# One SBUF tile with a table of places, and thirty groups of gates and values by seven products

## The chip, the cores and the metric

The kernel runs on one core of one Trainium2 chip. The metric is device time in microseconds. Before the change it is 280.34 us, the median of three runs (279.88 to 280.62). Half precision (f16) is used for most operands, PSUM sums are f32.

## What is computed

Attention over 4 sequences of 768 positions with 8 heads of 64, in which each query looks only at 6 of its 24 chunks of 32 keys, and then a gated feed-forward layer over the 3072 tokens:

```python
k_min, k_max = min and max of k over each chunk of 32 keys
ub = sum(maximum(q * k_min, q * k_max))          # bound of each chunk, future chunks at -1e9
top_chunks = argsort(ub)[..., -6:]
attn = softmax(where(chunk in top_chunks and causal, q @ k.T / sqrt(64), -1e9))
x = (attn @ v) as [3072, 512]
gate = sigmoid(x @ w_gate); val = x @ w_val      # 512 x 1536 each
out = (gate * val) @ w_out                       # 1536 x 512
```

## The kernel before, in words

The 24 blocks of 128 tokens are grouped into eight units (u0 to u7) of 384 tokens. For each unit the kernel prepares keys and queries (transposes, chunk minima and maxima, copies into `hk` and `hq`), chooses the chunks (`choose`), attends (`attend`: scores at line 937, exponentials at 948, the causal mask at 954, values at 970, then `finish` divides and turns the result into `xT`), and runs the feed-forward layer (`ffn`, line 1223). The feed-forward of one unit stands beside the attention of the next.

All work is registered with a planner (`Plan.add`) as steps with the engines they may run on. The order of all steps and the engine of each are written out in the string `ORDER`; `SLOTS` names for each buffer the slot it uses, and `TIES` adds waits, each of a GpSimd step for a VectorE step. `Plan.order` only reads these strings. Each engine runs its own steps in the order in which they stand.

`ffn` makes gates and values in groups of four feature blocks (`q4`), three groups of each a unit. The long way (`whole`, line 1230) is 4 matmuls of 384 columns for each feature block. Where `SEVEN` names the group, `by7` (line 1181) splits the 512 x 512 weights and the 512 x 384 inputs into halves and forms the four quarter results from seven products in place of eight (Winograd's form of Strassen's method):

```python
product("p7", side, ...); product("p1", lead, ...)
move("e7", side, f7); product("p4", side, ...)
move("e4", side, f4); move("sd", lead, side)
product("p6", lead, ...); onto("c21", f4); product("p2", side, ...)
product("p5", lead, ...); onto("c22", f7); product("p3", lead, ...)
```

`side` and `lead` are two PSUM banks. A product (line 1190) is 4 matmuls of 192 columns. `move` (line 432 or 434) copies a bank to SBUF or to the other bank, on ScalarE or VectorE; `onto` (line 1205) adds `lead` to `f4` or `f7` on VectorE. Products use sums of weights (`ss`, line 1158, four for each group's weights, made once) and differences of inputs (`tt`, line 1173, four a unit). Then come four tanh steps (`squash`, line 1243) for gates and four gating steps (`gated`, line 1249) for values. `SEVEN` holds the gates of unit 5 and the gates and values of units 6 and 7: 15 groups.

The last layer of units 4 to 7 (`pair`, line 1046) is by seven products too: once over two blocks of a unit, and once over the third blocks of two units (u45, u67; the earlier unit's third blocks are kept in `held`). Its sums lie in `sw` or `sx`, the weight sums in `tw` (line 1033), and the four result blocks in a part of `sw`, or for u45 and u67 in `ox`; they are scaled on the way (lines 1040, 1042, 1088) and stored (line 1110). Other units use the long way (`o`, line 1313).

SBUF buffers come from tile pools with a number of slots for each kind (line 415: 2 `big`, 6 `v`, 7 `np`, 9 `hg` and so on). Weight sums and differences have no slots of their own: they lie in areas whose first use is over (`homes`, `t_`, and the kind `nq`, which lies in `hk[0]`), and `done_with` adds the waits for the earlier use. `weight_sums` waits for the keys of sequence 3 (line 1403).

Of the kernel before, what the change touches and what calls it, by code (L numbers as in the profile page):

```python
# [14 lines left out]
NEG = -60000.0  # L15

# [22 lines left out]
class Plan:  # L39
# [3 lines left out]
    def __init__(self, slots, caps):  # L43
        self.slots, self.caps = slots, caps
        self.ops = []
        self.writer, self.readers = {}, {}
# [80 lines left out]
kx0_u2_1=V kx0_u2_3=V kx1_u2_3=V kx1_u2_2=V kx0_u2_2=V qm_u2_3=V kcr_u2=V ub_u2=P qf16_3=V kt_u2_3=A kf16_3=V osb_u0_1=A scf_3=P  # L127
expf_3_0=A out_u0_0=S vc_3=G hk1_u2_1=G hk0_u2_0=V hk0_u2_3=G kt_u2_2=A g_u1_1=P tanh_u1_1=A g_u1_0=P cmf_3_0=G ubn1_u2=V ubn0_u2=V
mx1_u2=V k11_1=S k00_1=S k10_1=S g_u1_8=P mx0_u2=V g_u1_4=P ap1_u2=V v_u1_0=P ap0_u2=V tanh_u1_4=A k01_1=S apt1_u2=V tanh_u1_0=A apt0_u2=V
expf_3_1=A hqm0_u2_0=A hqm1_u2_0=G v_u1_4=P v_u1_1=P sc_u2_4_1=P hg_u1_4=V q11_1=S sc_u2_5_2=P tanh_u1_8=A q01_1=S q10_1=S exp_u2_5_2=A  # L130
q00_1=S exp_u2_4_1=A pvf_3_0=P rzf_3_0=V out_u0_1=S cmf_3_1=G v16_0_5=G xf_3_0=V g_u1_5=P sc_u2_4_0=P sc_u2_1_2=P v16_0_4=G tanh_u1_5=A
sc_u2_5_1=P v_u1_5=P hg_u1_0=V hk1_u2_3=G pvf_3_1=P sc_u2_4_2=P sc_u2_5_0=P v_1_3=S hg_u1_1=V ss0_g0=V hqm0_u2_2=G exp_u2_4_0=A
sc_u2_0_2=P exp_u2_1_2=A rzf_3_1=V g_u1_3=P hq1_u2_2=G exp_u2_5_1=A sc_u2_1_0=P hg_u1_5=V xf_3_1=V exp_u2_5_0=A exp_u2_4_2=A g_u1_6=P
exp_u2_0_2=A hk0_u2_2=G kx1_1_2=V sc_u2_1_1=P xpsf_3_0=P kx0_1_1=V sc_u2_0_0=P o0_u0_2=P k16_1_3=A o1_u0_2=P v_1_0=S cm_u2_4=G
exp_u2_1_0=A sc_u2_0_1=P exp_u2_1_1=A kx0_1_3=V cm_u2_5=G exp_u2_0_0=A v_u1_3=P kx0_1_2=V kx1_1_1=V hqm1_u2_2=G hk1_u2_2=G sc_u2_6_2=P
tanh_u1_6=A k16_1_2=G o2_u0_2=P cm_u2_1=G cm_u2_0=G tanh_u1_3=A hg_u1_3=V sc_u2_6_0=P v_u1_6=P ss0_g1=G kx0_1_0=V exp_u2_0_1=A pv_u2_1=P
osb_u0_2=A g_u1_10=P hq0_u2_3=G ss1_g1=G kx1_1_0=V exp_u2_6_0=A kx1_1_3=V sc_u2_3_0=P hg_u1_6=V exp_u2_6_2=A v_u1_8=P pv_u2_0=P hg_u1_8=V
k16_1_0=G k16_1_1=A rz_u2_0=V g_u1_7=P exp_u2_3_0=A hq1_u2_3=G xTf_3_0=A kt_1_0=V x_u2_0=V qf0_u3_2=V k00_2=S sc_u2_3_1=P exp_u2_3_1=A
tanh_u1_7=A sc_u2_7_0=P pv_u2_5=P sc_u2_7_1=P sc_u2_2_2=P pv_u2_4=P k01_2=S kt_1_3=V sc_u2_7_2=P exp_u2_7_1=A k10_2=S sc_u2_2_1=P
qf0_u3_3=V v_u1_10=P exp_u2_7_0=A sc_u2_3_2=P rz_u2_2=V x_u2_2=V exp_u2_2_1=A g_u1_9=P kcr_1=G cm_u2_3=G exp_u2_2_2=A qf0_u3_0=V cm_u2_6=G  # L140
qf0_u3_1=V tanh_u1_10=A tanh_u1_9=A g_u1_2=P qm_u3_2=G exp_u2_3_2=A tanh_u1_2=A qf0_u4_1=V sc_u2_6_1=P v_u1_7=P g_u1_11=P v_u1_2=P
hq1_u3_0=G qm_u3_0=A kt_1_1=V hk1_1_0=G v_1_1=S v_u1_9=P exp_u2_7_2=A cm_u2_7=G ub_u3=P hg_u1_10=V hq1_u3_2=A hg_u1_7=V sc_u2_2_0=P
exp_u2_2_0=A v_u1_11=P exp_u2_6_1=A hg_u1_2=V o0_u1_2=P qf0_u4_0=V hk1_1_3=G xps_u2_2=P xpsf_3_1=P xT_u2_2=A v16_1_3=G o1_u1_2=P
hq0_u3_0=G ubn1_u3=V ubm1_u3=V cm_u2_2=G mx1_u3=V kt_1_2=V hg_u1_9=V pv_u2_7=P o0_u1_1=P ap1_u3=V apt1_u3=V pv_u2_3=P qf0_u4_2=V ubn0_u3=V
pv_u2_6=P pv_u2_2=P k11_2=S tanh_u1_11=A hg_u1_11=V xTf_3_1=A hk1_1_1=G hqm1_u3_0=A sc_u3_4_2=P hqm1_u3_2=A sc_u3_5_2=P exp_u3_5_2=A
# [12 lines left out]
tanh_u2_7=A hg_u2_9=V sc_u3_2_2=P exp_u3_2_2=A v_u2_1=P v_u2_3=P hk0_2_1=G ubn1_u4=V cm_u3_1=G sc_u3_3_2=P tanh_u2_10=A sc_u3_2_0=P
qf0_u5_2=V qm_u5_0=A rz_u3_2=V exp_u3_2_0=A ubn0_u4=V v_2_1=S sc_u3_3_0=P exp_u3_3_2=A hg_u2_1=V cm_u3_0=G cm_u3_2=G g_u2_3=P ubm0_u4=V
hk0_2_2=G pv_u3_0=P k11_3=S mx0_u4=V sc_u3_1_1=P exp_u3_1_1=A sc_u3_2_1=P exp_u3_3_0=A v_u2_7=P ap0_u4=V tanh_u2_3=A exp_u3_2_1=A v_u2_2=P  # L160
g_u2_6=P apt0_u4=V g_u2_5=P hg_u2_3=V hk1_2_1=G hqm0_u4_0=A tanh_u2_6=A v16_1_5=G cm_u3_3=G ubm1_u4=V v_u2_5=P hg_u2_2=V sc_u4_0_2=P
tanh_u2_5=A exp_u4_0_2=A v16_2_0=G hqm0_u4_2=G pv_u3_1=P x_u3_2=V hg_u2_7=V hq1_u5_0=G sc_u4_0_3=P exp_u4_0_3=A sc_u4_1_3=P v_u2_10=P
sc_u4_1_2=P k10_3=S hg_u2_5=V qm_u5_2=A v_u2_6=P sc_u4_0_1=P exp_u4_1_2=A rz_u3_0=V x_u3_0=V hg_u2_10=V sc_u4_1_0=P v16_2_1=G mx1_u4=V
sc_u4_0_0=P xT_u3_2=S exp_u4_1_0=A exp_u4_0_0=A exp_u4_0_1=A ap1_u4=V pv_u3_3=P sc_u4_2_3=P pv_u3_2=P rz_u3_1=V cm_u4_0=G sc_u4_2_0=P
x_u3_1=V exp_u4_1_3=A hk1_2_3=G hq1_u4_0=G o0_u2_0=P sc_u4_2_2=P xT_u3_1=S hg_u2_6=V exp_u4_2_3=A hq1_u4_2=G sc_u4_1_1=P exp_u4_2_0=A
sc_u4_3_0=P kx1_3_3=V pv_u4_0=P exp_u4_3_0=A apt1_u4=V kx0_3_0=V sc_u4_3_1=P exp_u4_1_1=A k16_3_2=G exp_u4_3_1=A qf0_u6_0=V ub_u5=P
ubn1_u5=V sc_u4_3_3=P cm_u4_1=G hqm1_u4_0=A v_3_3=S k16_3_0=G cm_u4_2=G sc_u4_3_2=P exp_u4_3_2=A sc_u4_2_1=P mx1_u5=V o1_u2_0=P o2_u2_0=P
exp_u4_2_2=A hqm1_u4_2=A ubn0_u5=V qf0_u6_3=V xT_u3_0=S osb_u2_0=V g_u3_0=P k16_3_1=G kt_3_0=V pv_u4_1=P sc_u4_7_3=P sc_u4_4_2=P g_u3_5=P
rz_u4_0=V exp_u4_3_3=A qf0_u6_1=V sc_u4_7_0=P sc_u4_7_2=P tanh_u3_0=A exp_u4_4_2=A sc_u4_4_1=P v_u3_0=P qf0_u6_2=V exp_u4_7_3=A cm_u4_3=G
# [212 lines left out]
def kernel(  # L382
# [741 lines left out]
    def flat(t):  # L1124
        return t.rearrange("p a s -> p (a s)")
# [221 lines left out]
    for i in range(3):  # L1347
        weights_out(i, 0.3, [])
# [113 lines left out]
```

## Time and profile before

| | |
|---|---|
| median of 3 runs | 280.34 us (279.88 to 280.62) |
| profiled execution | 279.69 us, span 277.9 us |
| TensorE (PE) / weight loads (PEld) | 266.3 / 195.8 us busy |
| VectorE (DVE) / ScalarE (ACT) / GpSimd (POOL) | 220.7 / 202.4 / 159.0 us busy |
| granted TensorE clock | 1.00 |

The profile shows one execution. The span runs from its first to its last instruction. A busy time is the time in which an engine has at least one instruction under way. Matmuls are pipelined, so a record (326 ns for a matmul of 384 columns) is longer than the time by which it moves the next one on. The chain is the work that ended last, followed back from the last instruction. A group of instructions gives line, engine, operation, output and input, count, then busy time, mean ns of one, and the engine's idle time just before them with its releaser.

### The profile page before, as it was taken

What the parts mean: (1) busy time and instruction counts of PE and PEld (TensorE: products, weight loads), DVE (VectorE), ACT (ScalarE), POOL (GpSimd) and SP (SyncE); (2) the same over time, 40 slices, a digit from 0 to 9 for tenths busy, and PEclk for the clock granted to TensorE, in tenths of its full rate; (3) what the DMA queues carried; (4) which work ended last, traced back from release to release, by engine and by line L of the source; (5) the groups of instructions that cost most, each with busy time, mean ns of one, the idle gap of its engine ahead of it and who ended that gap; (6) DMA issues with size and microseconds to landing.
All of it is one profiled execution on the core that took longest, in us unless ns stands there. A gap on an engine that the chain in (4) does not pass through costs nothing.

```text
span 277.9 us, 7782 instructions
## 1 busy us (share of the span) xinstructions
PE 266.3 (96%) x2914; PEld 195.8 (70%) x2914; DVE 220.7 (79%) x649; ACT 202.4 (73%) x436; POOL 159.0 (57%) x254
## 2 busy tenths in 40 slices
PE   6968999999999999999999999999999999999993
PEld 4744658666756566757667656767986899999982
DVE  4798845769989998999896889557868568879872
ACT  6387869659777877888886998767877695576441
POOL 5797644648778666884847545531553765251621
PEclk9999999999999999999999999999999999999999
DMA  7999999999998999958843205300302030010315
GB/s 160 242 270 198 201 215 214 211 192 188 206 191 180 193 216 179 163 113 173 139 108 88 80 0 120 92 0 2 96 4 78 0 84 17 0 40 1 116 42 188
DMA packets 131574, 34.72 MB, mean 125 GB/s; under 512 B 119760, under 2 KB 128464, under 8 KB 131536
## 3 DMA queue, kind: packets, MB, share of 16 engines
q1 hardware_dynamic: 126768, 29.50, 50.4%
q0 software_dynamic: 4768, 4.72, 10.1%
q8 instruction: 23, 0.38, 0.6%
q14 instruction: 15, 0.12, 0.1%
HBM read 30.67 MB, written 6.29 MB: 133 GB/s over the span
## 4 chain that ended last, share of the span: by engine, by line
PE 88%; DMA 6%; POOL 1%; SPq 1%; ACT 1%; DVE 1%; issue 0%; DVEq 0%; ACTq 0%
PE v_u L1236 16%; PE g_u L1236 14%; PE sc_u L937 13%; PE o_u L1313 11%; PE pv_u L970 7%; PE pl_g_u L1190 4%; PE pl_u L1065 4%; PE ps_u L1065 4%; PE ps_g_u L1190 3%; PE ube_u L876 3%; DMA wg<-in_moe_w_gate_dram 3%; PE pl_v_u L1190 3%; PE ps_v_u L1190 2%; DMA out_dram<-ox 1%; DMA qf<-in_q_dram 1%; SPq L616 1%
## 5 line engine op out<-in xcount | busy, mean ns | idle before, releaser
L948 ACT ACTIVATE att_u<-sc_u 128x512 f16<-128x512 f32 (+3 forms) x184 | 91.0, 552 | 17.2 <-PE sc_u L937 12.6
L1236 PE MATMUL v_u<-xT_u,wv 128*128 128x384 f16 x288 | 55.6, 326 | 0.0
L1236 PE MATMUL g_u<-xT_u,wg 128*128 128x384 f16 x240 | 46.7, 326 | 1.7 <-DMA wg<-in_moe_w_gate_dram 0.8
L954 POOL TENSOR_SCALAR_AFFINE_SELECT att_u<-att_u 128x384 f16<-128x384 f16 (+1 forms) x56 | 27.9, 508 | 28.9 <-ACT att_u L948 16.8
L1249 DVE SCALAR_TENSOR_TENSOR hg_u<-gate_u,v_u 128x384 f16<-128x384 f16 x60 | 32.2, 543 | 14.8 <-PE v_u L1236 6.6
L1243 ACT ACTIVATE gate_u<-g_u 128x384 f16<-128x384 f32 x60 | 29.1, 500 | 13.4 <-PE g_u L1236 13.1
L1236 PEld LDWEIGHTS <-wv 128*128 128x128 f16 x288 | 27.2, 98 | 14.5 <-issue 0.2
L1313 PE MATMUL o_u<-wo,hg_u 128*128 128x512 f16 x144 | 35.0, 379 | 0.0
L1236 PEld LDWEIGHTS <-wg 128*128 128x128 f16 x240 | 22.0, 98 | 14.9 <-DMA wg<-in_moe_w_gate_dram 2.5
L937 PE MATMUL sc_u<-hqo,hko 128*128 128x128 f16 (+2 forms) x220 | 29.2, 243 | 0.0
L937 PE MATMUL sc_u<-hqe,hke 128*128 128x128 f16 (+2 forms) x220 | 28.7, 243 | 0.0
L970 PE MATMUL pv_u<-v,att_u 128*128 128x65 f16 x640 | 27.4, 193 | 0.0
L970 PEld LDWEIGHTS <-att_u 128*128 128x128 f16 x640 | 25.1, 98 | 2.9
L937 PEld LDWEIGHTS <-hke 128*128 128x128 f16 x220 | 17.2, 98 | 6.9 <-issue 2.0
L1313 PEld LDWEIGHTS <-hg_u 128*128 128x128 f16 x144 | 13.4, 98 | 12.1
L937 PEld LDWEIGHTS <-hko 128*128 128x128 f16 x220 | 16.8, 98 | 5.8 <-issue 0.4
L653 POOL CAST v<-v 128x512 f16<-128x512 f32 x23 | 14.1, 613 | 7.7 <-PE sc_u L937 2.6
L991 DVE TENSOR_TENSOR x_u<-pv_u,rz_u 128x384 f16<-128x384 f32 (+1 forms) x28 | 14.8, 529 | 0.4
L1205 DVE TENSOR_TENSOR f_g_u<-pl_g_u,f_g_u 128x384 f32<-128x384 f32 x18 | 9.9, 553 | 4.0 <-PE pl_g_u L1190 3.6
L1190 PEld LDWEIGHTS <-ss 128*128 128x128 f16 x144 | 12.4, 98 | 0.7
L899 DVE MAX8 mx_u<-ubn_u 128x8 f32<-128x8 f32 (+16 forms) x152 | 12.6, 158 | 0.1
L1055 POOL TENSOR_TENSOR sw<-hg_u 128x256 f16<-128x256 f16 x7 | 4.7, 670 | 13.6 <-DVE hg_u L1249 8.0
(246 smaller groups left out, 612.7 us busy)
## 6 DMA issues: line engine op xcount, KB each, us to landing
v<-in_v_dram SPq DMA_DIRECT2D x23, 256.0 KB, 3.6
k<-in_k_dram SPq DMA_DIRECT2D x12, 384.0 KB, 5.4
q<-in_q_dram SPq DMA_DIRECT2D x12, 384.0 KB, 5.6
out_dram<-osb_u SPq DMA_DIRECT2D x12, 256.0 KB, 2.9
out_dram<-sw SPq DMA_DIRECT2D x8, 256.0 KB, 2.2
wv<-in_moe_w_val_dram POOLq DMA_DIRECT2D x3, 512.0 KB, 10.7
wo<-in_moe_w_out_dram POOLq DMA_DIRECT2D x3, 512.0 KB, 17.8
qf<-in_q_dram SPq DMA_DIRECT2D x8, 128.0 KB, 3.4
```

Source lines behind the costliest of these rows:

```text
L653: plan.add(f"v16_{b}_{ib}", {POOL: pool(H * D)}, lambda e: nc.gpsimd.tensor_copy(v16[b % 2][:, ib, :, 0:D], at(t)), reads=[t], writes=[("v ...
L937: nc.tensor.matmul(at(t)[:, o:o + 128 * m], hk[b % 2][e_][:, p, 128 * jb:128 * jb + 128], hq[u.side][e_][:, p, 128 * x:128 * (x + m)], sta ...
L948: plan.add(f"exp_{u.name}_{h}_{y}", {ACT: act(n)}, lambda e, t=t, att=att, b0=b0, n=n: nc.scalar.activation(at(att)[:, b0:b0 + n], at(t), ...
L954: nc.gpsimd.affine_select(out=dv, in_=dv, compare_op=ALU.is_ge, fill=0.0, base=0, pattern=[[0, u.m], [1, 128]], channel_multiplier=-1)
L970: nc.tensor.matmul(at(pv)[:, last, x, :], at(att)[:, c:c + 128], v16[b % 2][:, jb, h, :], start=(jb == 0), stop=(jb == ib))
L991: plan.add(f"x_{u.name}_{p}", {DVE: dve(u.t)}, lambda e: nc.vector.tensor_tensor(at(x_).rearrange("p a (e d) -> p e a d", e=2), at(pv)[:, ...
L1065: nc.tensor.matmul(at(to), a(j)[:, i], b(j)[:, i], start=first and j == i == 0, stop=j == 2 and i == 1, skip_group_check=True)
L1190: nc.tensor.matmul(at(to)[:, s], a()[:, c, 128 * s:128 * s + 128], b()[:, c], start=first and s == c == 0, stop=c == 1, skip_group_check=True)
L1236: nc.tensor.matmul(at(t), w16[:, c, 128 * fb:128 * fb + 128], at(u.xt)[:, c, :], start=(c == 0), stop=(c == 3))
L1243: made = plan.add(f"tanh_{u.name}_{name}", {ACT: act(T, psum)}, lambda e: nc.scalar.activation(dst(), src(), AF.Tanh, scale=0.5), reads=re ...
L1249: plan.add(f"hg_{u.name}_{name}", {DVE: dve(T)}, lambda e: nc.vector.scalar_tensor_tensor(dst(), gate(), 1.0, src(), ALU.add, ALU.mult), r ...
L1313: nc.tensor.matmul(at(o), at(hgs[fc // 2])[:, fc % 2, 128 * tb:128 * tb + 128], wo16[:, fc, lo:hi], start=(fc == 0), stop=(fc == NFB - 1))
```

## The change

All passing SBUF buffers become ranges of one tile, the arena: 234 places of 256 f16 elements a partition, and `SLOTS` gives each buffer its first place. PSUM buffers stay as they are. Ranges may be used one after the other by buffers of any kind. `ss`, `tt`, `held`, `sums`, `four` and the gates of the seven products are now buffers of their own; the areas in `hk`, `hq`, `v16`, the explicit waits (`done_with`, the wait of `weight_sums`), and the shared `sw`, `sx`, `ox` are gone. `att` buffers take as much as their unit needs.

`SEVEN` grows from 15 groups to 30: gates and values of units 3, 4 and 5 are added where they were missing.

`ORDER`, `SLOTS` and `TIES` are written anew; the first 425 entries of `ORDER` are the same. Steps by engine, before and after: PE 686 and 731, DVE 503 and 538, ACT 435 and 471, POOL 248 and 260, SP 127 and 127. Ties: 163 and 190. The order of `tw` (weight sums of the last layer), registered earlier, is in `ORDER` still at units 4 and 5; the 24 steps of `ss` end in it before the products of unit 4. The copies `move` are on VectorE 9 times of 45 before and 22 of 90 after.

```diff
-    plan = Plan(
-        {"ps": 8, "big": 2, "v": 6, "np": 7, "qf": 2, "qm": 1, "kx": 2, "kt": 3, "ubn": 1, "mx": 1, "apt": 1,
-         "att": 4, "rz": 2, "x": 3, "xt": 2, "gate": 4, "hg": 9, "osb": 2, "nq": 6},
-        {("ps", "ff"): 4, ("ps", "sc"): 3, ("ps", "pv"): 2, ("ps", "pr"): 3, ("ps", "ub"): 2},
-    )
+    plan = Plan()
+    UNIT = 256
+    arena = land.tile([128, UNITS * UNIT], F16, tag="arena", name="arena")

     def at(b):
...
+            t = arena[0:b.shape[0], UNIT * b.slot:UNIT * b.slot + n * (2 if b.dtype == F32 else 1)]
+            if b.dtype == F32:
+                t = t.bitcast(F32)
...
-            att = Buf("att", f"att_{u.name}_{h}", [128, 1920], F16)
+            att = Buf("att", f"att_{u.name}_{h}", [128, 128 * len(u.where)], F16)
...
-    tw = Buf("big", "tw", [128, 4, 3, 2, 256], F16)
-    sw = Buf("big", "sw", [128, 3072])
-    held = Buf("qm", "held", [128, 2, NFB, 128], F16)
-    sx = Buf("qf", "sx", [128, 3, 4, 2, 128], F16)
-    ox = Buf("qf", "ox", [128, 4, 256])
+    tw = Buf("tw", "tw", [128, 4, 3, 2, 256], F16)
...
-    def pair(name, block, keys, sums, four, skey, okey, rows, next_):
+    def pair(name, block, keys, rows, next_):
...
+        skey = Buf("sums", f"sums_{name}", [128, 3, 4, 2, 128], F16)
+        okey = Buf("four", f"four_{name}", [128, 4, 256])
...
-    SEVEN = {5: {"g": (0, 1, 2)}, 6: {"g": (0, 1, 2), "v": (0, 1, 2)}, 7: {"g": (0, 1, 2), "v": (0, 1, 2)}}
+    SEVEN = {3: {"g": (0, 1, 2), "v": (0, 1, 2)}, 4: {"g": (0, 1, 2), "v": (0, 1, 2)}, 5: {"g": (0, 1, 2), "v": (0, 1, 2)}, 6: {"g": (0, 1, 2), "v": (0, 1, 2)}, 7: {"g": (0, 1, 2), "v": (0, 1, 2)}}
...
     for m in "gv":
         for i in range(3):
+            b = Buf("ss", f"ss_{m}{i}", [128, 4, 512], F16)
+            ss[m, i] = [((b, x), lambda b=b, x=x: at(b)[:, x]) for x in range(4)]
...
+        tt = Buf("tt", f"tt_{u.name}", [128, 4, 2, T2], F16)
...
-                gate = [Buf("nq", f"gq_{u.name}_{2 * q4 + f}", [128, 2, T], F16) for f in range(2)]
+                gate = [Buf("gq", f"gq_{u.name}_{2 * q4 + f}", [128, 2, T], F16) for f in range(2)]
...
+                u.held = Buf("held", f"held_{u.name}", [128, NFB, 128], F16)
...
+    weight_sums(0.4)
     prepare(units[1], 0.0, 0.8)
...
-    summed = weight_sums(4.9)
     attend(units[4], 4.0)
...
-    turned_k = [op for op in plan.ops if op.name.startswith("kt_3_")]
-    for op in summed:
-        op.deps += [(d, False) for d in turned_k]
```

At the end of the kernel the pairs run interleaved: unit 6, unit 7 and u67. Before, the last matmuls are those of u67; after, those of unit 7. In the new `SLOTS` the results `four` of u45 stand at place 214 and those of u67 at 198, eight places each.

More of the change, by code (lines that the diff above doesn't have):

```diff
@@ L130 @@
[L130 to L133, printed above, removed]
@@ L1042, in halved, with sums, four @@
             nc.vector.tensor_scalar_mul(o, i, 0.5)
-    def pair(name, block, keys, sums, four, skey, okey, rows, next_):
+    def pair(name, block, keys, rows, next_):
         EV = 0.1
+        skey = Buf("sums", f"sums_{name}", [128, 3, 4, 2, 128], F16)
+        okey = Buf("four", f"four_{name}", [128, 4, 256])
+        def sums(n, j):
+            return at(skey)[:, j, n]
+        def four():
+            return at(okey)
         for j in range(3):
@@ L1112, in store @@
             dma=((hi - lo) * 1.35, 2048 if hi - lo > 256 else 512))
[L1114 removed]
+    SEVEN = {3: {"g": (0, 1, 2), "v": (0, 1, 2)}, 4: {"g": (0, 1, 2), "v": (0, 1, 2)}, 5: {"g": (0, 1, 2), "v": (0, 1, 2)}, 6: {"g": (0, 1, 2), "v": (0, 1, 2)}, 7: {"g": (0, 1, 2), "v": (0, 1, 2)}}
     T2 = T // 2
[L1116 to L1136 removed]
     ss = {}
[L1138 to L1139 removed]
+    for m in "gv":
+        for i in range(3):
+            b = Buf("ss", f"ss_{m}{i}", [128, 4, 512], F16)
+            ss[m, i] = [((b, x), lambda b=b, x=x: at(b)[:, x]) for x in range(4)]
     made7 = set()
@@ L1147, in halves, with xt_keys @@
         return lambda: view().rearrange("p (i f) -> p i f", i=2)
+    def xt_keys(u):
+        return [(u.xt, c) for c in range(4) if u.m] + [(u.xt, c, x) for c in range(4) for _, x in u.first]
     def sums_of(u, next_):
@@ L1172, in sums_of @@
                                     (lambda: x_(1, 1), lambda: x_(0, 1)), (lambda: x_(1, 0), lambda: t_(1)))):
-            made = plan.add(f"tt{n}_{u.name}", {DVE: dve(384, 2), POOL: pool2(384)}, lambda e, a=a, b=b, n=n: both(e).tensor_tensor(
-                t_(n), a(), b(), ALU.subtract), reads=[(u.xt, c) for c in range(4)] + [(tk, n // 2)] * (n % 2), writes=[(tk, n)], port=True, prio=next_())
-            done_with(made, keys0 if u.i == 5 else [("hq", u.side, 0, n), ("hqm", u.side, 0, n), ("hqm", u.side, 0, n, "zero")])
-        return t_, x_
+            plan.add(f"tt{n}_{u.name}", {DVE: dve(384, 2), POOL: pool2(384)}, lambda e, a=a, b=b, n=n: both(e).tensor_tensor(
+                t_(n), a(), b(), ALU.subtract), reads=xt_keys(u) + [(tt, n // 2)] * (n % 2), writes=[(tt, n)], port=True, prio=next_())
+        return t_, x_, tt
     def by7(u, m, i, next_, views):
-        t_, x_ = views
+        t_, x_, tt = views
         name = f"{m}{i}_{u.name}"
@@ L1206, in onto @@
                      reads=[lead, f], writes=[f], prio=next_(0.1))
-        xs = [(u.xt, c) for c in range(4)]
+        xs = xt_keys(u)
         product("p7", side, sum_(2), lambda: t_(2), tk(2, 2), True)
@@ L1227, in ffn @@
         hgs = []
-        xt = [(u.xt, c) for c in range(4) if u.m] + [(u.xt, c, x) for c in range(4) for _, x in u.first]
+        xt = xt_keys(u)
         def whole(m, fb):
@@ L1242, in squash @@
         def squash(name, src, dst, psum, reads, writes):
[L1243 to L1246 removed]
+            plan.add(f"tanh_{u.name}_{name}", {ACT: act(T, psum)}, lambda e: nc.scalar.activation(dst(), src(), AF.Tanh, scale=0.5),
+                     reads=reads, writes=writes, prio=next_(EV))
         def gated(name, gate, src, dst, psum, reads, writes):
```

529 lines of the change are left out of this document (265 added, 264 removed).

## The prediction

> **What bounds the kernel now.** I read the page first, then the stretches of 20 us, then the chain. A busy TensorE alone proves little, since its records overlap, so the pace within the chain decides.
>
> ```profile
> span 277.9 us, 7782 instructions
> PE 266.3 (96%) x2914; PEld 195.8 (70%) x2914; DVE 220.7 (79%) x649; ACT 202.4 (73%) x436; POOL 159.0 (57%) x254
> PE   6968999999999999999999999999999999999993
> PE 88%; DMA 6%; POOL 1%; SPq 1%; ACT 1%; DVE 1%; issue 0%; DVEq 0%; ACTq 0%
> ```
>
> ```profile
> 60.00:80.00 20.00, 20.00 (x189) 13.80 (x188) 18.10 (x35) 17.77 (x39) 14.70 (x25) 1.00 1.13 193
> 80.00:100.00 20.00, 20.00 (x194) 11.91 (x192) 18.29 (x55) 14.34 (x31) 15.82 (x25) 1.00 1.06 195
> 100.00:120.00 20.00, 20.00 (x270) 14.00 (x269) 18.58 (x66) 16.99 (x37) 13.91 (x22) 1.00 0.85 161
> 120.00:140.00 20.00, 20.00 (x241) 13.17 (x237) 18.94 (x59) 16.83 (x36) 14.29 (x21) 1.00 0.78 148
> 140.00:160.00 20.00, 20.00 (x256) 13.35 (x255) 16.46 (x63) 16.16 (x30) 11.65 (x17) 1.00 0.39 96
> 160.00:180.00 20.00, 20.00 (x236) 13.07 (x234) 16.54 (x56) 16.76 (x32) 10.92 (x15) 1.00 0.31 74
> 180.00:200.00 20.00, 20.00 (x221) 15.15 (x219) 14.14 (x38) 14.65 (x32) 6.61 (x11) 1.00 0.11 29
> 200.00:260.00 60.00, 60.00 (x706) 54.25 (x704) 46.61 (x117) 43.39 (x104) 26.53 (x40) 1.00 0.10 30
> 260.00:278.00 18.00, 13.20 (x126) 11.72 (x123) 10.31 (x30) 4.90 (x14) 6.75 (x11) 0.99 0.33 125
> ```
>
> The columns are length, busy PE, PEld, DVE, ACT and POOL with their instructions, granted clock, DMA share and GB/s. From 60 to 260 us TensorE is busy all the time at a granted clock of 1.00, and 88% of the chain is TensorE. VectorE is second: 90 to 95% in the stretches from 60 to 140 us. ScalarE reaches 89%, GpSimd 79%. After 200 us only TensorE is full. The DMA transfers stand in the chain at the head and in the tail.
>
> ```profile
> 212.98 2.60 PE v_u L1236 x16
> 215.58 0.66 PE ps_g_u L1190 x8
> 216.24 0.22 PE sc_u L937 x2
> ```
>
> These are three neighbours in the chain: start, length, line and number of matmuls. 212.98 + 2.60 = 215.58 and 215.58 + 0.66 = 216.24: one piece starts where the other ends, and TensorE waits for nobody. So a matmul of 384 columns costs 2.60 / 16 = 0.163 us of TensorE and one of 192 columns 0.66 / 8 = 0.0825 us, and each microsecond of matmuls taken out is a microsecond of the end, as long as TensorE stays fed.
>
> **The change part by part.**
>
> *Products.* Four feature blocks of gates or values for 384 tokens take 16 matmuls of 384 columns (L1236): 16 x 0.1625 = 2.60 us. By seven products they take 28 of 192 columns (L1190): 28 x 0.0825 = 2.31 us. That is 0.29 us less for each group. SEVEN grows from 15 groups to 30: six of unit 3, six of unit 4, the three value groups of unit 5. 15 x 0.29 = 4.35 us leave TensorE (240 long matmuls out, 420 short ones in). All 15 lie in the stages where TensorE is full: **minus 4.35 us**.
>
> *What the products need around them.* Each group has two additions on VectorE (c21, c22; L1205) and three moves out of PSUM (e7, e4, sd; ScalarE or VectorE). The tanh and the gating stay four each, of 384 elements a partition.
>
> ```profile
> L1205 DVE TENSOR_TENSOR f_g_u<-pl_g_u,f_g_u 128x384 f32<-128x384 f32 x18 | 9.9, 553 | 4.0 <-PE pl_g_u L1190 3.6 <-ACT ox L1040 0.3
> L434 DVE COPY f_g_u<-ps_g_u 128x384 f32<-128x384 f32 x3 | 1.7, 554 | 0.2 <-PE ps_g_u L1190 0.2
> L1158 DVE TENSOR_TENSOR ss<-wg x5: 408/418/426, 64.4 to 190.2; 128x512 f16<-128x512 f16 x5
> L1173 DVE TENSOR_TENSOR hqe<-xT_u,hqe 128x384 f16<-128x384 f16 x3 | 1.1, 353 | 0.0
> ```
>
> The order that is written out names the engine of every step, so it can be counted. VectorE goes from 503 steps to 538. It gains 30 additions (30 x 0.553 = 16.6 us), 13 moves (22 instead of 9; 13 x 0.554 = 7.2 us) and 3 differences of x (11 instead of 8; 1.1 us). It loses 7 weight sums to GpSimd (11 instead of 18; 7 x 0.418 = 2.9 us) and, net, 4 smaller copies, about 2 us. Sum: about 20 us more for VectorE. ScalarE goes from 435 to 471:
>
> ```profile
> L432 ACT COPY f_g_u<-ps_g_u 128x384 f32<-128x384 f32 x15 | 7.0, 482 | 6.4 <-PE ps_g_u L1190 6.2 <-ACT hke L1243 0.2
> L1158 POOL TENSOR_TENSOR ss<-wg x1: 1149/1149/1149, 69.7 to 69.7; 128x512 f16<-128x512 f16 x1
> ```
>
> 32 more moves on it are 32 x 0.482 = 15.4 us. GpSimd goes from 248 to 260, with seven more sums of 1.149 us (8.0 us); it is the idlest of the four, and its 27 more ties (190 instead of 163, each a GpSimd step that waits for a VectorE step) hold up only GpSimd's own queue.
>
> *Is that covered?* From 60 to 200 us VectorE is busy 18.10 + 18.29 + 18.58 + 18.94 + 16.46 + 16.54 + 14.14 = 121.05 us of 140. With 20 us more it is 141.0 of 140 - 4.35 = 135.65. Taken as they stand, 5.4 us have no room: the upper end of the cost. But a record's last part is overlapped by the next record:
>
> ```profile
> 99.55 0.97 DVE L827 STREAM_TRANSPOSE kt<-k 128x768 f16<-128x768 f16 x1
> 100.44 0.94 DVE L661 TRANSPOSE_TENSOR_REDUCE kx<-k 128x24 f32<-128x768 f32 x1
> ```
>
> The second starts 0.08 us before the first ends. For the 372 instructions of the seven stretches that is up to 30 us that the busy time counts twice or as a tail, so the room is there, and the lower end is 0. It isn't below nothing: TensorE has no idle time there that a better order could take away. The nearest row is 120 to 140 us: VectorE 18.94 of 20 and TensorE still 20.00. That speaks for the lower end; that a whole stage of 135 us would now look like its fullest stretch speaks against exactly 0. I take **plus 1.0 us**, a fifth of the upper end.
>
> *The places.* Buffers that were rotating tiles are now ranges of one tile, given by the table. No byte is moved more: 127 SyncE steps before and after. The first 425 entries of the order are unchanged, which covers the head, so I count the places at nothing there. A write to a range that is still read has to wait, as it had to wait for a tile; the cover is the same as above. Weight sums used to wait for dead areas (line 1403 for keys, done_with for others); now all 24 of `ss` stand in the order ahead of unit 4's products. That moves work, and its cost is in the counts.
>
> *The tail.* One wait is removed, and here the profile shows it:
>
> ```profile
> 269.76 4.04 DMA out_dram<-ox
> 272.38 0.82 PE L1065 MATMUL pl_u<-wo,sx 128*128 128x256 f16 x6
> 273.90 0.43 DVE L1042 TENSOR_SCALAR ox<-ps_u 128x256 f32<-128x256 f32 x1 [1.81 <-DMA out_dram<-ox]
> 273.91 0.38 ACT L1040 ACTIVATE ox<-pl_u 128x256 f32<-128x256 f32 x1 [1.55 <-DMA out_dram<-ox]
> 274.39 0.33 SPq L1110 DMA_DIRECT2D out_dram<-ox  x1
> ```
>
> The pairs u45 and u67 share the buffer ox. The last two evacuations must wait until the store of u45 has read it, at 273.80, though the last matmul ends at 273.20. After the change the four blocks of u45 lie at places 214 to 221 and those of u67 at 198 to 205, which do not meet. What is late next is the last matmul itself: 273.20, then about 0.1 to start, 0.38 for the copy, 0.1 to the issue, and 277.9 - 274.39 = 3.51 from issue to the end, which gives 277.29 instead of 277.9: **minus 0.6 us**. (The order now ends with unit 7 in place of u67, with the same kinds of step.)
>
> *Sum.* The profiled execution took 279.69 us, of which 277.9 is its span. 279.69 - 4.35 - 0.6 + 1.0 = 275.74, which is 3.95 less. The median of the three runs is 280.34, 0.65 above the profiled one; 280.34 - 3.95 = **276.4 us**.
>
> [...]
>
> **The rivals.**
>
> *VectorE becomes the bound.* For it: the 141.0 of 135.65 above. Against it: the overlap of its records, and that its next largest jobs, the key extremes and transposes of 0.95 us, are needed a stage later. If the 5.4 us all come through: 279.69 - 4.95 + 5.4 = 280.1, against the median 280.8. No gain.
>
> *The hand-offs get uncovered (slower).* Two PSUM banks serve a group, and TensorE may not refill one before e7, e4, sd, c21 or c22 has emptied it: five hand-offs a group, 75 more. One that nothing covers costs the rest of the last matmul's record and the copy, 0.246 - 0.0825 + 0.482 = 0.65 us:
>
> ```profile
> L1190 PE MATMUL pl_g_u<-hqe,ss 128*128 128x192 f16 x48 | 5.9, 246 | 0.0
> L1190 PEld LDWEIGHTS <-ss 128*128 128x128 f16 x144 | 12.4, 98 | 0.7
> ```
>
> It decides from 4.95 / 75 = 0.066 us a hand-off on average, that is, when one in ten stands bare. With 15% bare it is 75 x 0.15 x 0.65 = 7.3 us: 279.69 - 4.95 + 7.3 = 282.0, median 282.7. For it: in units 3 and 4 the copies queue on a VectorE and a ScalarE that are far fuller than after 200 us. Against it: most of the groups of today run from 200 to 260 us, and TensorE is busy 60.00 of 60 there, with an idle time before L1190 of 0.0; and units 3 and 4 have scores and values of the next unit to run in between.
>
> *Weight loads set the pace.* If each short matmul had to wait for its load of 98 ns, a group would take 28 x 0.098 = 2.74 us, 0.14 more than the long way: 279.69 + 15 x 0.14 - 0.6 + 1.0 = 282.2, median 282.8. Against it stands 0.66 us for eight of them, and loads that overlap. [...]
>
> **How the numbers follow.** Forecast (products shorter, nearly all covered, tail wait gone), 275.0 to 278.6: 0.78. More than forecast, down to 274.6 or below: 0.02. VectorE the bound, about 280.8: 0.08. Hand-offs bare, about 282.7: 0.10. Weight loads, about 282.8: 0.02. The range of 274.5 to 279.4 leaves out the last three, under 2 in 10, and reaches from no cost of the cover (275.4) with some room to four times the cost taken. A difference of 0.3% (0.84 us) is about what a measurement can tell from no change. Faster by more than that 0.81, within it 0.07, slower 0.12: the forecast, the larger gain and an eighth of the VectorE case are faster, the rest of that case is about the same, and the other two are slower.
>
> **What would show it.** In the changed profile: L1236 left with 288 matmuls and the line of the seven products with 840, eight of these still in 0.66 us; TensorE busy 20.00 in every stretch from 60 us to some 4 us earlier than now; VectorE near 240 us in all, with stretches at 19 and more; no wait of an evacuation for a store of the four blocks in the last 5 us. The forecast is wrong if TensorE shows idle time before the products, released by VectorE or ScalarE copies (hand-offs), or if the key transposes come late and scores wait for them (VectorE the bound), or if loads of weights from the new places space the matmuls wider than 0.0825 us.

## The result, and the profile after

After the change the kernel takes **291.19 us**, the median of four runs (289.58 to 293.07), against 280.48 of the kernel before on the same chip: a ratio of 1.038 (95% interval 1.030 to 1.046). The forecast was 276.4. The kernel became slower by 10.7 us where 3.95 less were forecast. Of the kernels in this document some executions last over 1.5% longer than the fastest of the same kernel (one of the kernel with eleven copies on ScalarE took 951.96 us): the ratios leave these out, the medians keep them.

The page of the changed kernel, the lines that answer to those of before; the row with q1 is the queue of the loads, with packets, megabytes, and packet time as a share of 16 engines' span:

```profile
span 287.9 us, 8342 instructions
PE 268.6 (93%) x3094; PEld 208.1 (72%) x3094; DVE 235.8 (82%) x684; ACT 220.3 (77%) x472; POOL 171.6 (60%) x266
PE   5889999999779999988999989999999999999995
q1 hardware_dynamic: 126768, 29.50, 61.4%
```

The same queue before:

```profile
q1 hardware_dynamic: 126768, 29.50, 50.4%
```

Three things are to be seen. VectorE (235.8 us, from 220.7), ScalarE (220.3, from 202.4) and GpSimd (171.6, from 159.0) carry 15.1, 17.9 and 12.6 us more; the prediction counted about 20, 15.4 and 8.0. TensorE has holes in slices 11, 12, 18, 19 and 24 of the 40, where before stood only nines. And the same 126768 packets with the same 29.50 MB took 0.614 x 287.9 = 176.8 us a DMA engine, against 0.504 x 277.9 = 140.1: **26% more time for the same bytes**. Nothing in the prediction has a place for that.

The stretches after, with the columns of the prediction's table:

```profile
60.00:80.00 20.00, 18.44 (x159) 12.17 (x157) 13.87 (x33) 16.72 (x35) 11.76 (x20) 1.00 1.23 139
80.00:100.00 20.00, 17.91 (x186) 10.00 (x185) 17.02 (x55) 14.13 (x29) 12.50 (x18) 0.91 1.25 158
...
120.00:140.00 20.00, 17.64 (x202) 12.12 (x200) 15.83 (x67) 16.51 (x36) 12.03 (x18) 1.00 0.76 151
```

From 60 to 140 us TensorE loses most, and VectorE is *less* busy there than before (13.87 against 18.10 of 20 in the first row, 15.83 against 18.94 in the last). So VectorE isn't the bound; everybody waits. From 60 to 100 us the loads bring 139 and 158 GB/s where they brought 193 and 195, at a higher DMA share. The issue of the same loads on SyncE's queue (start, length, four transfers of 384 KB), first after, then before:

```profile
54.71 8.84 SPq L660 DMA_DIRECT2D arena<-in_k_dram  x4
63.59 11.53 SPq L660 DMA_DIRECT2D arena<-in_q_dram  x4
```

```profile
54.85 7.43 SPq L637 DMA_DIRECT2D k<-in_k_dram  x4
62.40 8.11 SPq L637 DMA_DIRECT2D q<-in_q_dram  x4
```

They start at the same time, and to issue all eight takes 20.4 us instead of 15.5. What follows is a chain of three engines, in the timeline after (81 to 85 us) and in its waits (total, times, longest; columns of the timeline: start, length, instruction, idle time before it and its releaser):

```profile
80.42 0.81 PE L1244 MATMUL v_u<-arena,wv 128*128 128x384 f16 x4
...
81.10 2.28 DVE L866 STREAM_TRANSPOSE arena<-arena 128x384 f32<-128x384 f32 x5 [2.61 <-issue]
...
83.30 0.52 DVE L1255 SCALAR_TENSOR_TENSOR arena<-arena,v_u 128x384 f16<-128x384 f16 x1
...
83.87 0.38 PE L960 MATMUL sc_u<-hqe,hke 128*128 128x256 f16 x2 [1.88 <-DVE arena L1255]
...
84.46 1.44 PE L1244 MATMUL v_u<-arena,wv 128*128 128x384 f16 x4 [0.21 <-ACT arena L455]
```

```profile
DVE arena L866 <- DMA arena<-in_q_dram: 3.6, 2, 2.1
```

VectorE stands idle for 2.61 us before the transposes of queries (L866). This row names no releaser ("issue" only). The four loads of `q` were issued from 63.59 to 75.12 us and landed 8.2 to 8.7 us after their issue, the last of them at about 81 us, just before the transposes start; and the other two waits of L866, in the row of the waits, are put down to such a load. So I read it as a wait for `q`. The gating (L1255) is queued behind the transposes; TensorE waits 1.88 us for the PSUM bank that the gating empties. And then four matmuls of 384 columns take 1.44 us, where four took 0.81 us at 80.42. The granted clock behind the idle time was 0.50:

```profile
85.00:87.00 2.00, 2.00 (x27) 0.69 (x33) 1.93 (x4) 1.36 (x3) 1.94 (x4) 0.50 1.17 135
```

### The profile page after: what moved, and what is told of

Read it like the earlier page. It is cut to its first block, busy times and chain, and to the rows that moved or that the text cites. A ratio compares the mean times of both kernels' runs of the same rounds, so it can differ in the third digit from the quotient of the medians.

```text
span 287.9 us, 8342 instructions
## 1 busy us (share of the span) xinstructions
PE 268.6 (93%) x3094; PEld 208.1 (72%) x3094; DVE 235.8 (82%) x684; ACT 220.3 (77%) x472; POOL 171.6 (60%) x266
## 3 DMA queue, kind: packets, MB, share of 16 engines
q1 hardware_dynamic: 126768, 29.50, 61.4%
## 4 chain that ended last, share of the span: by engine, by line
PE 39%; DVE 6%; DMA 4%; SPq 2%; issue 1%; ACT 0%; DVEq 0%
PE pl_v_u L1198 6%; PE pl_u L1092 5%; PE pl_g_u L1198 5%; PE ps_u L1092 4%; PE sc_u L960 4%; PE ps_v_u L1198 4%; PE ps_g_u L1198 4%; PE o_u L1319 3%; DMA arena<-in_q_dram 3%; PE pv_u L993 3%; SPq L660 2%; DMA arena<-arena 1%; DVE arena L1255 1%; DVE arena L1213 1%; DVE arena L850 1%
## 5 line engine op out<-in xcount | busy, mean ns | idle before, releaser
L971 ACT ACTIVATE arena<-sc_u 128x512 f16<-128x512 f32 (+3 forms) x184 | 90.0, 555 | 7.9 <-PE sc_u L960 5.4
L1198 PEld LDWEIGHTS <-arena 128*128 128x128 f16 x480 | 40.2, 98 | 5.3 <-issue 2.4
L1082 POOL TENSOR_TENSOR arena<-arena 128x256 f16<-128x256 f16 x36 | 23.8, 674 | 25.3 <-DVE arena L1082 14.1
L977 POOL TENSOR_SCALAR_AFFINE_SELECT arena<-arena 128x384 f16<-128x384 f16 (+1 forms) x56 | 27.9, 508 | 16.6 <-ACT arena L971 6.1
L1319 PE MATMUL o_u<-wo,arena 128*128 128x512 f16 x144 | 35.5, 379 | 0.2 <-DVE arena L1255 0.2
L1244 PE MATMUL v_u<-arena,wv 128*128 128x384 f16 x144 | 28.3, 331 | 0.7 <-ACT arena L1328 0.5
L1244 PE MATMUL g_u<-arena,wg 128*128 128x384 f16 x144 | 27.2, 326 | 1.0 <-ACT arena L455 0.7
L993 PE MATMUL pv_u<-v,arena 128*128 128x65 f16 x640 | 26.5, 193 | 0.0
L993 PEld LDWEIGHTS <-arena 128*128 128x128 f16 x640 | 24.3, 98 | 2.1 <-POOL arena L977 0.2
L1092 PEld LDWEIGHTS <-arena 128*128 128x128 f16 x252 | 23.9, 98 | 2.3
L1255 DVE SCALAR_TENSOR_TENSOR arena<-arena,v_u 128x384 f16<-128x384 f16 x36 | 18.9, 540 | 7.4 <-ACT arena L1251 5.6
L1198 PE MATMUL pl_g_u<-arena 128*128 128x192 f16 x180 | 22.2, 246 | 1.1 <-DVE arena L1213 1.1
L1319 PEld LDWEIGHTS <-arena 128*128 128x128 f16 x144 | 13.4, 98 | 11.8 <-issue 0.4
L1198 PE MATMUL pl_v_u<-arena 128*128 128x192 f16 x180 | 21.5, 246 | 0.0
L1244 PEld LDWEIGHTS <-wg 128*128 128x128 f16 x144 | 13.3, 98 | 9.2 <-DMA wg<-in_moe_w_gate_dram 1.5
```

The source lines that it names most:

```text
L971: plan.add(f"exp_{u.name}_{h}_{y}", {ACT: act(n)}, lambda e, t=t, att=att, b0=b0, n=n: nc.scalar.activation(at(att)[:, b0:b0 + n], at(t), ...
L977: nc.gpsimd.affine_select(out=dv, in_=dv, compare_op=ALU.is_ge, fill=0.0, base=0, pattern=[[0, u.m], [1, 128]], channel_multiplier=-1)
L993: nc.tensor.matmul(at(pv)[:, last, x, :], at(att)[:, c:c + 128], v16[b % 2][:, jb, h, :], start=(jb == 0), stop=(jb == ib))
L1082: plan.add(f"sw{n}_{name}_{j}", {DVE: dve(256, 2), POOL: pool2(256)}, lambda e, a=a, b=b, op=op, n=n, j=j: both(e).tensor_tensor(sums(n, j ...
L1092: nc.tensor.matmul(at(to), a(j)[:, i], b(j)[:, i], start=first and j == i == 0, stop=j == 2 and i == 1, skip_group_check=True)
L1198: nc.tensor.matmul(at(to)[:, s], a()[:, c, 128 * s:128 * s + 128], b()[:, c], start=first and s == c == 0, stop=c == 1, skip_group_check=True)
```

## The theories

**A, the base address.** The tables count places from the start of the arena, but the arena itself starts where the program puts it: behind the lone tiles, at byte 72000 of each partition, which is 281 x 256 + 64. Every landing buffer is then 64 bytes past a multiple of 256. Before, the landing buffers started at multiples of 256 (53760 and 66048, for instance). `k` and `q` land in pieces of 128 bytes, `v` in pieces of 256. If pieces that lie across a multiple of 128 bytes land slower, the slow loads are explained by the address alone. **B, the load of the engines** (the rivals of the prediction): VectorE and ScalarE are too full in units 3 to 5, buffers come free late, and the loads only look slow.

## The experiments

**The arena on a multiple of 256 bytes.** One unused tile ahead of it moves the arena by 192 bytes:

```diff
+    pad = lone("pad", [128, 96])
```

> The kernel after, with 192 unused bytes a partition ahead of the arena, so that it starts at byte 72192 (a multiple of 256) instead of 72000 (64 past one). No step, wait or order differs. Theory A, the loads land off their 256-byte lines and come late, and VectorE's queue waits for them: the four loads of q_1, issued in 11.5 us after and 8.1 us before, are back at about 8 us, the idle time of TensorE from 60 to 140 us (6.6 us) is gone for the most part, and the time is 276 to 279 us. Theory B, VectorE and ScalarE are simply too full in units 3 to 5: the loads may get faster, but the time stays at 288 to 292 us.

277.93 us, ratio 0.990 (0.987 to 0.992): 13 us less than the change as it stands. The queue's row on the page of this kernel (span 275.4 us), and the issue of the loads of `q`:

```profile
q1 hardware_dynamic: 126768, 29.50, 50.8%
```

```profile
62.94 9.41 SPq L661 DMA_DIRECT2D arena<-in_q_dram  x4
```

```profile
60.00:100.00 40.00, 40.00 (x389) 1.00 1.07 184
```

The order, the places and every instruction are the same. The packets take 0.508 x 275.4 = 139.9 us again, as before the change; the loads of `q` are issued in 9.41 us, not quite in the 8 expected. From 60 to 100 us TensorE (the number behind the comma) is busy all the time again, as it is from 100 to 140 and from 140 to 180. B can't be the main cause.

The pad moves the whole arena and the weights behind it, so steps of the engines and stores might have become faster too. The profiles say no. Matmuls of the output (`o_u`) take 379 ns in both on average, the gating of `v_u` 540 and 543. Of the transfers, with their number, size and median time from issue to landing, the loads of `k` and `q` changed and the stores hardly, first in the changed kernel, then with the pad:

```profile
out_dram<-arena SPq DMA_DIRECT2D x24, 256.0 KB, 2.6
arena<-in_k_dram SPq DMA_DIRECT2D x12, 384.0 KB, 8.2
```

```profile
out_dram<-arena SPq DMA_DIRECT2D x24, 256.0 KB, 2.4
arena<-in_k_dram SPq DMA_DIRECT2D x12, 384.0 KB, 5.9
```

With this, A is shown.

**The kernel before, shifted by 64 bytes.**

```diff
+    pad = head.tile([128, 32], F16, tag="pad", name="pad")
```

> The kernel before, with 64 unused bytes a partition ahead of its landing buffers, so that they start 64 past a multiple of 256 as the arena does. Theory A: the four loads of q_1 take 11 to 12 us instead of 8.1; the kernel before has the loads earlier against their use and a less full VectorE, so it loses something between 1 and 8 us (281 to 288 us). Theory B: within 0.5 us of the kernel before.

292.07 us, ratio 1.041 (1.037 to 1.046). The shift alone makes the *old* kernel, which has none of the change, as slow as the changed one, more than was expected. The profiled execution is the longest of the six (295.09 us, span 293.4); its packets take 58.8% of 16 engines' span, 172.5 us against 140.1:

```profile
65.41 11.94 SPq L638 DMA_DIRECT2D q<-in_q_dram  x4
```

(The pad stands ahead of everything here, and so moves all SBUF buffers, not the landing buffers alone.)

**The arena 128 bytes past a multiple of 256.** As the first, with 32 elements in place of 96.

> The kernel after, with 64 unused bytes, so that the arena starts at byte 72064 (128 past a multiple of 256). Pieces of 128 bytes (k and q) then lie within one 256-byte line, those of 256 bytes (v) across two. If 128-byte alignment is what counts: k and q loads as fast as with 256, time within 1 us of that run. If every piece has to start on a 256-byte line: loads as slow as after, 288 to 292 us. Theory B: 288 to 292 us either way.

278.78 us, ratio 0.992 (0.989 to 0.995), the same as on a multiple of 256:

```profile
62.70 9.49 SPq L661 DMA_DIRECT2D arena<-in_q_dram  x4
```

So what counts for the 128-byte pieces is a multiple of 128 bytes, not of 256: the loads of `q` are issued in 9.49 us here, against 9.41 on a multiple of 256 and 11.53 at 64 past one. The packets take 52.8% of 277.3, 146.4 us, some 5% more than on a multiple of 256: the pieces of `v`, of 256 bytes, now lie across a multiple of 256, and their loads land in 4.2 us in place of 3.9.

**The loads alone.** Sets of four loads into one tile, at shifts of 0, 64, 128, 192, 32, 0, 64 and 128 bytes:

```diff
+    for i, shift in enumerate((0, 64, 128, 192, 32, 0, 64, 128)):
+        lo = shift // 4
+        t = room[:, lo:lo + 3072].rearrange("a (p c d) -> a p c d", p=NP, c=NC)
...
+        nc.vector.tensor_copy(first[:, 2 * i:2 * i + 1], room[:, lo:lo + 1])
```

> Only loads: no attention and no gate, value or output product is computed; the outputs are zeros. Eight sets of four loads of 384 KB (pieces of 128 bytes, as k and q of one batch) go to one tile at 0, 64, 128, 192, 32, 0, 64 and 128 bytes past a multiple of 256, each set closed by a small VectorE copy; then eight sets of four loads of 256 KB (pieces of 256 bytes, as v) at the same shifts. Theory A (the place of the landing piece within its 128 bytes sets the pace): the sets of 128-byte pieces at 64, 192 and 32 take 25 to 50% longer than those at 0 and 128 (about 11 us against 8 us); the sets of 256-byte pieces take longer at every shift but 0. Theory B (the loads were slow because of what else ran beside them): all sets of one kind agree within 5%.

The copies that close the sets:

```profile
16.27 0.15 DVE L35 COPY first<-room 128x1 f32<-128x1 f32 x1 [10.44 <-DMA room<-in_k_dram]
28.22 0.15 DVE L35 COPY first<-room 128x1 f32<-128x1 f32 x1 [11.79 <-DMA room<-in_q_dram]
36.27 0.15 DVE L35 COPY first<-room 128x1 f32<-128x1 f32 x1 [7.89 <-DMA room<-in_k_dram]
48.39 0.15 DVE L35 COPY first<-room 128x1 f32<-128x1 f32 x1 [11.97 <-DMA room<-in_q_dram]
62.61 0.15 DVE L35 COPY first<-room 128x1 f32<-128x1 f32 x1 [14.06 <-DMA room<-in_k_dram]
72.99 0.15 DVE L35 COPY first<-room 128x1 f32<-128x1 f32 x1 [10.23 <-DMA room<-in_q_dram]
85.28 0.15 DVE L35 COPY first<-room 128x1 f32<-128x1 f32 x1 [12.13 <-DMA room<-in_k_dram]
93.00 0.15 DVE L35 COPY first<-room 128x1 f32<-128x1 f32 x1 [7.57 <-DMA room<-in_q_dram]
```

The idle time before a copy is the time of its set. Three sets (1st, 5th, 6th) were issued only when the queue had drained and hold a whole landing; the others follow close on the set before. Like with like: drained, 10.4 and 10.2 us at 0 against **14.1 at 32**; close behind, 7.9 and 7.6 at 128 against **11.8 and 12.1 at 64 and 12.0 at 192**. That is 36% (one set at 32) and about 55% more, with no other engine at work. The sets of 256-byte pieces care less: 6.6 and 6.0 us at 0, 6.7 to 6.9 elsewhere.

The aligned arena is 0.990 of the kernel before, and 0.986 was forecast. Where is the rest? TensorE's waits after 60 us in the aligned kernel (total, times, longest); before the change this answer is empty:

```profile
PE ps_v_u L1199 <- DVE arena L1256: 0.5, 1, 0.5
PE pl_g_u L1199 <- DVE arena L1214: 0.4, 1, 0.4
PE sc_u L961 <- DVE hqo L457: 0.2, 1, 0.2
PE o_u L1320 <- DVE arena L1256: 0.2, 1, 0.2
```

All four wait for VectorE. (Profiles of other executions show a fifth wait; see the repeat below.) Is VectorE too full? Three runs ask, all on the aligned arena.

**Thin additions.** In the 15 new groups the additions c21 and c22 write 8 of 192 columns:

```diff
-nc.vector.tensor_tensor(at(f), at(lead), at(f), ALU.add)
+nc.vector.tensor_tensor(at(f)[:, :, 0:n], at(lead)[:, :, 0:n], at(f)[:, :, 0:n], ALU.add)
```

> The arena on a multiple of 256 bytes, and in the 15 groups that are new to the seven products the two wide VectorE additions write 8 of 192 columns instead of all (the rest of the sum is left out), so VectorE has some 13 us less to do; all instructions and waits stay. If the extra VectorE work is what eats about 2 us of the products' gain (cover lost): 275.5 to 276.5 us against 277.9 of the aligned arena. If the lost time lies in the hand-offs or in the order, not in VectorE: 277.5 to 278.2.

276.37 us, ratio 0.989 (0.986 to 0.991). The time fits the first theory, but the kernel before was faster too when run beside it (279.49 us against 280.25), and by the ratio there is little change (0.990 without the edit). VectorE fell only to 226.6 us, 9.3 less, since a thin addition still takes 0.165 us. So the time doesn't decide. Of the waits the first two are still there:

```profile
PE ps_v_u L1199 <- DVE arena L1257: 0.8, 1, 0.8
PE pl_g_u L1199 <- DVE arena L1215: 0.4, 1, 0.4
```

**Eleven copies to ScalarE.** e7, e4 and sd of units 5 to 7 that stood on VectorE change their letter in `ORDER` (`e7_g0_u5=V` to `=A`, and ten more).

> The arena on a multiple of 256 bytes, and the eleven PSUM copies of units 5 to 7 that VectorE did (about 0.55 us each, 6 us) go to ScalarE, which is the less busy of the two from 180 us on. If the two remaining gaps of TensorE at 199 and 230 us (0.6 us each) come from a full VectorE queue: 276.7 to 277.5 us. If they come from the order itself, or ScalarE's queue makes the copies late: 277.8 to 279.

279.13 us, ratio 0.998 (0.995 to 1.001): worse than the aligned arena. The first of the old waits stays (0.9 us), and ScalarE's queue makes a new one:

```profile
PE ps_g_u L1199 <- ACT ps_g_u L455: 0.9, 1, 0.9
```

**One product twice.**

```diff
-                for s in range(2):
+                for s in (0, 1, 0, 1) if twice and p == "p7" else range(2):
```

> The arena on a multiple of 256 bytes, and the first product of each of the 15 new groups is issued twice (60 more matmuls of 192 columns at 0.0825 us, 4.95 us of TensorE more; the result is the same). If TensorE is the bound nearly everywhere: 277.9 + 4.9 = 282.8 us. If 2 us of its time is waiting for VectorE, part of the addition lies in those waits: 280.5 to 281.5.

281.17 us, ratio 1.005 (1.003 to 1.007), 1.1 to 1.5 points above the aligned arena (0.994 and 0.990 on two chips), which is 3.1 to 4.2 of the 4.95 us added. It lies between the two theories: TensorE is the bound nearly everywhere, and a part of the addition fell into its waits.

The amount of VectorE's work so explains little of the loss. The timeline of the aligned arena shows another cause at each of the gaps:

```profile
182.39 1.33 POOL L1053 TENSOR_TENSOR arena<-wo 128x512 f16<-128x512 f16 x1
182.74 1.20 DVE L457 COPY hqo<-arena 64x768 f16<-64x768 f16 x1
```

```profile
196.17 1.15 POOL L1053 TENSOR_TENSOR arena<-wo,arena 128x512 f16<-128x512 f16 x1
196.47 1.26 DVE L1256 SCALAR_TENSOR_TENSOR arena<-arena 128x384 f16<-128x384 f16 x1
197.99 1.15 POOL L1053 TENSOR_TENSOR arena<-wo,arena 128x512 f16<-128x512 f16 x1 [0.66 <-DVE arena L1013]
198.20 1.09 DVE L1083 TENSOR_TENSOR arena<-arena 128x256 f16<-128x256 f16 x1
199.81 0.49 PE L1199 MATMUL pl_g_u<-arena 128*128 128x192 f16 x4 [0.44 <-DVE arena L1214]
```

```profile
229.91 0.56 DVE L1256 SCALAR_TENSOR_TENSOR arena<-arena,ps_v_u 128x384 f16<-128x384 f16 x1 [1.11 <-DMA arena<-arena]
230.52 0.49 PE L1199 MATMUL ps_v_u<-arena 128*128 128x192 f16 x4 [0.49 <-DVE arena L1256]
```

At 182, 196 and 198 us a VectorE step that usually takes 0.35, 0.55 or 0.28 us takes 1.20, 1.26 or 1.09: it ends only after the weight sum of the last layer (`tw`) that GpSimd had begun. Four gating steps of this profile have both inputs in SBUF and start behind a GpSimd sum (196.47, 235.92, 251.32 and 252.09 us), and each ends 0.41 or 0.42 us after that sum's end; a gating step that takes its value from PSUM keeps its 0.55 us beside such a sum (219.62 us). The changed kernel's profile has the same: four gating steps with both inputs in SBUF that start behind a GpSimd sum or difference take 1.26, 0.99, 0.84 and 1.02 us (208.78, 248.39, 263.79 and 264.56 us) and end 0.41 or 0.42 us after its end, and one with its value in PSUM takes 0.54 us (161.62 us). By what means GpSimd holds VectorE up, the profiles don't show. At 229 us it is a place: the gating writes `hg_u6_0` at place 66, where `x_u7_0` lies, which a DMA transpose is still reading. Two small edits follow.

**The aligned arena again,** with the edit of the first run, beside these two on the same chip.

> The kernel with the arena on a multiple of 256 bytes once more, beside the next two on the same chip: 0.990 of the kernel before, as the first time, on every theory.

277.88 us, ratio 0.994 (0.992 to 0.997). On this chip the gain is 0.4 points smaller than on the first one. The profile of this execution has the four waits again, and one more, which the first profile of the same kernel lacks:

```profile
PE sc_u L961 <- ACT arena L972: 1.3, 1, 1.3
```

```profile
154.32 5.00 ACT L972 ACTIVATE arena<-sc_u 128x512 f16<-128x512 f32 x10 [1.51 <-DMA arena<-arena]
```

TensorE waits for the exponentials, and these for a DMA transpose. By `ORDER` and `SLOTS` it is a place again: the exponential that comes next writes places 54 and 55 (`att_u5_1` starts at 52), where `x_u4_1` lies, which the transpose reads. The wait stands in the profiles of the arena at 128 bytes (1.4 us) and of the thin additions (1.1) too, and not in those of the next two runs. The four transposes there took 7.19, 6.15 and 7.00 us of the queue where it stands, and 5.33 us in the first profile of the aligned arena, where it doesn't.

**Two places.**

```diff
-x_u7_0:66
+x_u7_0:98
...
-x_u7_1:16
+x_u7_1:95
```

> The aligned arena, and two buffers of unit 7 (x_u7_0 and x_u7_1, read by DMA transposes) at places of their own (98 and 95 instead of 66 and 16), so that the gating no longer writes where a transpose still reads. If the gap of 0.65 us at 229.5 us is the wait for that place: it goes, and the time falls by 0.3 to 0.7 us against the aligned arena. If it is VectorE's full queue: no change (within 0.2 us), and the gating of that step starts as late as before.

276.75 us, ratio 0.990 (0.987 to 0.992), 1.1 us less than the aligned arena beside it, more than expected. How much of it the two places brought isn't separated: the wait at 229 us was 0.5 to 0.8 us, and the wait for the exponentials comes and goes between executions. The wait at 229 us is gone, two gating steps now run back to back:

```profile
227.50 1.12 DVE L1256 SCALAR_TENSOR_TENSOR arena<-arena,ps_v_u 128x384 f16<-128x384 f16 x2
```

**Two places, and three sums on VectorE.**

```diff
-tw2_0=G
+tw2_0=V
...
-tw1_1=G
+tw1_1=V
...
-tw3_1=G
+tw3_1=V
```

(their three ties go too).

> As the run with two places, and three weight sums (tw2_0, tw1_1, tw3_1) go from GpSimd (1.15 to 1.33 us each) to VectorE (0.42 us each). If the gaps of TensorE at 184 and 199 us come from VectorE steps that last twice as long while GpSimd works on such a sum (1.20, 1.26 and 1.09 us instead of 0.54, 0.55 and 0.28): they go, and the time falls by a further 0.5 to 1.2 us. If they come from the amount of VectorE work: the 1.26 us more make them longer, and the time rises by 0 to 0.8 us.

**275.42 us, ratio 0.985** (0.983 to 0.987), a further 1.3 us less. VectorE has 1.26 us of work more and the gaps are gone all the same: the answer on TensorE's waits after 60 us is empty, and

```profile
196.33 0.55 DVE L1256 SCALAR_TENSOR_TENSOR arena<-arena 128x384 f16<-128x384 f16 x1
180.00:200.00 20.00, 20.00 (x279) 17.77 (x276) 18.96 (x47) 18.51 (x42) 10.57 (x16) 1.00 0.22 56
```

the gating takes 0.55 us again, the copy that took 1.20 us takes 0.36, and TensorE is busy 20.00 of 20 us in the stretch where these gaps lay. This version beats the kernel before by 1.5% and the change as it stands by 5%.

## Why the prediction was wrong, point by point

*The places.* This is the step that failed: "No byte is moved more ... so I count the places at nothing". No byte more was moved, but the bytes of the short pieces moved slower, because the new tile starts 64 bytes off. It cost 291.19 - 277.93 = 13.3 us (the kernel before took 280.48 and 280.25 beside these two), more than all that the rest of the change brings. The argument stopped at the table and the order and didn't ask at which byte the table starts. The sentence on ranges ("A write to a range that is still read has to wait ... the cover is the same") failed as well, in a small way: there is no such wait of TensorE in the kernel before after 60 us, and two in the aligned arena, at place 66 (0.5 to 0.8 us) and, in some executions, at places 54 and 55 (1.1 to 1.4 us).

*Products.* Right. Eight short matmuls still move the next piece by 0.66 us, as in the chain of the aligned arena:

```profile
131.01 0.66 PE pl_g_u L1199 x8
```

The rival of weight loads, 28 x 0.098 us a group, is out.

*The cover.* The size was too small, and the reason incomplete. The count itself is off: VectorE has 15.1 us more, not 20; GpSimd 12.6, not 8.0, since five more of the differences `tt` went to it (9 steps instead of 4, 0.91 us each), which the prediction left out. The amount of VectorE's work is covered, as forecast: in the last run it is busy 18.96 of 20 us from 180 to 200 us, and no wait of TensorE for it is left. What was not covered is *when* single steps run: the aligned arena is 1.7 to 2.9 us faster than before (ratios 0.994 and 0.990) where products and tail give 4.35 + 1.3 = 5.6, so 2.7 to 3.9 us were lost instead of the 1.0 taken. The last two edits bring back 2.5 of it (277.88 to 275.42). The prediction said of GpSimd's added ties that they "hold up only GpSimd's own queue"; a GpSimd step that runs beside a VectorE step can hold up VectorE as well (1.26 us instead of 0.55 at 196.47 us of the aligned arena).

*The tail.* Right in kind, too small in size. The last matmul and the last copy of the aligned arena:

```profile
271.59 0.38 PE L1093 MATMUL ps_u<-wo,arena 128*128 128x256 f16 x2
272.00 0.38 ACT L1060 ACTIVATE arena<-ps_u 128x256 f32<-128x256 f32 x1 [6.13 <-PE ps_u L1093]
```

No copy waits for a store any more. From the last matmul's end to the end of the span it is 275.4 - 271.97 = 3.4 us instead of 4.7, so 1.3 less in place of 0.6. Where the other 0.7 came from wasn't followed up.

*The rivals.* None of them was what happened. "The hand-offs get uncovered" had the right sign and nearly the right kind of chain, TensorE waiting for a bank, but in the slow kernel the copies were late because VectorE stood still for a load. "VectorE becomes bound" is refuted by the stretches, in which it is less busy than before. With the arena on a multiple of 256 bytes, two places moved and three sums on VectorE, the change is worth 279.68 - 275.42 = 4.3 us, and the forecast's sum was 3.95. That the two are so close is luck in part: the tail brought 0.7 more than counted, and products and tail together, 5.6, are still 1.3 above 4.3, with no wait of TensorE after 60 us to explain it. The mechanism of the gain was right; what was missing was the cost of the address.

Left open are this last 1.3 us, and why the shift by 64 bytes costs the kernel before about as much (1.041) as the changed one (1.038; the intervals overlap), though its VectorE is less full. No run moved the landing places alone inside a whole kernel; that it is the loads rests on the loads alone and on the profiles, in which the stores and the engines' steps keep their times.

## What to carry to other kernels

When buffers move into one hand-placed tile, work out the byte at which that tile starts, and keep the landing place of every load with short pieces on a multiple of the piece: here 64 bytes decided 13 us. Compare packet time for equal bytes in the queue's row before looking for a busy engine. And when a full engine seems to be the cause, look for a step that lasts twice its usual time or more, and for what ran beside it, before moving work to another engine.

## What the runs showed of the hardware

- Loads in 128-byte pieces took 36 to 55% longer when the pieces lay across a multiple of 128 bytes in SBUF, with nothing else at work: 14.1 us a set at a shift of 32, against 10.2 and 10.4 at 0, and 11.8 to 12.1 at 64 and 192, against 7.6 and 7.9 at 128 bytes past a multiple of 256. With 256-byte pieces a shift of 32 to 192 bytes cost less: 6.7 to 6.9 us in place of 6.0 and 6.6.
- A gating step on VectorE with both inputs in SBUF lasted 1.26 us instead of 0.55 when a GpSimd sum of 1.15 us began before it. Such a step with one input in PSUM kept its 0.55 us.
- Behind an idle time of 1.88 us TensorE's granted clock was 0.50 from 85 to 87 us in the profile of the changed kernel, and four matmuls took 1.44 us in place of 0.81. That the idle time lowered the clock isn't shown: behind an idle time of 1.08 us in the same profile (76 to 78 us) and behind the wait of 1.3 us in the repeat of the aligned arena (154 to 162 us) it stayed at 1.00, and from 16 to 20 us of the changed kernel, where the longest wait in the 4 us before was 0.99 us, it was 0.53 and 0.61.
